# First loads on two queues, a shorter GpSimd chain for the second layer norm, and a new order for all engines

## The chip, the cores and the metric

The kernel runs on one core of a Trainium2 chip. The metric is the device time of one execution in microseconds (us). In the traces and below, PE is the matrix engine (TensorE; its weight loads are shown apart as PEld), DVE is VectorE, ACT is ScalarE, POOL is GpSimd, and SP is the engine that issues most of the transfers. An entry such as "SPq" or "ACTq" is that engine's transfer queue.

## The reference, cut to what matters

One transformer layer over 2048 tokens of width 640, in bfloat16. The first half is linear attention with 32 heads of 20 columns. Its feature map is a softmax of `p` beside a softmax of `-p`, where `p` is q or k times a small weight for each head.

```python
x = A_x
h = x + attention(layernorm(x), wqkv, w_phi, wo)
h2 = h + silu(layernorm(h) @ w1) @ w2          # 640 -> 1728 -> 640

def attention(x, wqkv, w_phi, wo):
    q, k, v = split(x @ wqkv)                  # 32 heads of 20
    phi(y)  = concat(softmax(y @ w_phi), softmax(-(y @ w_phi)))   # 40 features
    kv, z   = phi(k).T @ v, sum(phi(k))        # over all 2048 tokens
    return ((phi(q) @ kv) / (phi(q) @ z + 1e-6)) @ wo
```

The sum `kv` over all tokens cuts the work in two: no query can be finished before the last key is done.

## The kernel before, in words

The 2048 tokens are 16 tiles of 128, numbered t = 0 to 15. Nothing loops: the whole program is one list of words, `ORDER`, and every engine issues its instructions in the order in which the words stand there. A word is an operation and its arguments. `kp.1@2` is the key projection of tile 1 into the PSUM banks from bank 2 on; PSUM has 8 banks, and an operation that takes a bank waits until what lay there has been read out. A letter at the end picks an engine: `a` is ACT and `v` is DVE for a copy or a normalisation; `s` and `a` pick SP's or ACT's queue for a load; for `kn`, `p` gives the whole tile to POOL, `q` three quarters and `b` half, the rest going to DVE.

The start. `lx`, `lk`, `lv`, `lp` load tiles of x, chunks of the key weight, the value weight and the small weight (line 233). `wm` are matmuls on zeros without use for the result (L261). `wt.c` transposes chunk c of the key weight on PE (L312), `wc.c` copies it out (L166 on DVE, L168 on ACT), `fk.c` multiplies it with the small weight (L327), and `fc.c` copies the product to `Wfk`. All five chunks have to be there before a `kp` can end. `lq`, `gk`, `gc` are the same for the query weight, with transposing loads (L248). `st` (L266, L267) and `rs` (L270 to L279) give mean and reciprocal deviation of a tile, `xn` the normalised tile (L287 on DVE, L292 on ACT). It is transposed either by PE (`xt`, L298, copied out by `xc`) or by a transposing transfer on SP (`xd`, L305).

Stage one, tiles in any order: `vp` and `kp` project (L360, ten matmuls each), `vc` copies v out (L168), `ke` takes exp(p) and exp(-p) on ACT (L385), `kr` sums and inverts on DVE (L393, L396), `kn` normalises (L403 on POOL, L407 on DVE), `cc` accumulates kv in bank 7 (L416). `kc`, `km` and `mt` turn kv into a block-diagonal matrix.

Stage two: `qp.g.i` projects queries of four tiles (L447, ten matmuls of 512 columns, five where i is 2), `qe` takes the exponentials (L457). `dp.t` multiplies with kv (L482), always into four banks; `dw.t` reads them out on DVE in four instructions (L495, L496, L498, L501), `dr` inverts (L506), `do` divides, half a tile at a time, on POOL or DVE (L512), `td` transposes (L532), `op` projects (L539), `oa` adds x on DVE with the row sums (L548). The second layer norm is `sq` (squares and their sums on ACT, L556), `sr` (a chain of one-column steps on POOL, L561 to L569), `hn` (L575), and `hd`, the transposing transfer (L595).

Stage three: for groups of 2, 4, 4, 4 and 2 tiles, `up` projects to 1728 columns (L610, L620), `ua` is the silu on ACT (L632), `yp` and `yh` project back (L656, L669), and `yo` adds the residual and stores (L677, L681). The last tile, 13, is stored in two parts, `yz` (L686).

Of the kernel before, what the change touches and what calls it, by code (L numbers as in the profile page):

```python
# [8 lines left out]
AF = mybir.ActivationFunctionType  # L9
ALU = mybir.AluOpType  # L10
# [8 lines left out]
F32 = mybir.dt.float32  # L19
# [3 lines left out]
WHERE = {t: (g, i) for g, ts in enumerate(GROUPS) for i, t in enumerate(ts)}  # L23

ORDER = """
mo lx.0.1.s st.0 lk.2.3.s wm.512@7 wm.512@7 wm.512@7 wm.512@7 wm.512@7 wm.512@7 wt.2@0 lp.a mk ph lk.3.4.s
wm.256@2 wm.256@2 wm.256@2 wt.3@1 ta wc.2.a wc.3.a lx.1.2.s wm.256@4 wm.256@4 wm.256@4 fk.2@2 lk.0.1.s
wt.0@4 fc.2.a fk.3@6 fc.3.a st.1 rs.0.1 xn.0.v lk.1.2.s wt.1@5 xt.0@0 xc.0.a lk.4.5.s wt.4@1 wc.0.v fk.0@2
fc.0.a wc.1.v fk.1@6 wc.4.v fk.4@4 lx.2.4.s rs.1.2 xn.1.v st.2 xt.1@0 lx.12.16.s st.12 fc.1.a lv.0.3.s st.13
fc.4.a wm.256@1 wm.256@1 wm.256@1 wm.256@1 kp.0@2 xc.1.a kp.1@6 lv.3.5.s rs.2.3 xn.2.a xt.2@1 lx.8.12.s  # L30
lx.4.8.s ke.0 lh.s rs.12.14 xn.12.a xd.12 xn.13.a st.14 vp.1@4 vc.1.a ke.1 xc.2.v kp.2@2 vp.2@0 ke.2 vc.2.a
st.15 rs.14.16 st.8 st.9 xn.15.v xd.13 rs.8.10 xn.9.a vp.0@4 kp.12@6 ke.12 kp.13@2 xn.14.v st.5 st.4 rs.4.6
xn.5.a vc.0.a st.11 xd.15 vp.15@0 lq.3.s vc.15.a xd.14 kp.15@6 ke.15 vp.12@4 l1.2.s xn.4.a vc.12.a vp.13@0
vc.13.a vp.14@6 st.10 rs.10.12 st.7 st.6 rs.6.8 ke.13 xn.11.v xd.11 gk.3@4 xn.10.v xd.5 xd.10 vc.14.a
kp.14@0 kr.1 lq.1.s ke.14 mc gc.3.a xn.7.a xn.6.a kr.0 vp.5@2 vc.5.a kn.1.p vp.10@6 st.3 kp.11@0 vp.11@4
xd.9 kp.5@2 xn.8.a vc.11.a rs.3.4 xn.3.a kr.13 kr.14 vc.10.a kr.12 kp.10@4 kn.0.q cc.0 ke.5 kn.13.q cc.13
ke.11 kr.15 cc.1 kn.14.p cc.14 xd.4 kp.4@2 kn.15.p kr.5 kn.5.b xt.3@6 ke.10 xd.8 vp.8@0 kp.8@4 xc.3.a ke.4
vc.8.a lq.2.s kr.11 xd.6 vp.6@2 vc.6.a kr.2 lq.0.s gk.0@0 kr.4 ke.8 cc.5 kn.12.q gc.0.a kr.8 cc.15 kn.11.p
vp.9@2 vc.9.a kn.4.p xd.7 kp.7@4 ke.7 kr.7 gk.1@0 kn.8.q gc.1.a vp.4@2 vc.4.a kn.2.p kp.9@4 ke.9 kr.9 kn.9.b
lq.4.s gk.4@0 gc.4.a kr.10 vp.7@2 vc.7.a cc.4 cc.8 vp.3@4 vc.3.a gk.2@0 gc.2.a kp.3@2 ke.3 kr.3 kp.6@4 ke.6  # L40
lo.s qp.0.2@6 qe.0.2 qp.0.0@0 qe.0.0 qp.0.1@2 qe.0.1 kr.6 cc.9 l2.4.8.s kn.7.p cc.7 kn.10.b cc.10 kn.3.p
cc.3 cc.2 cc.12 cc.11 kn.6.q cc.6 mt close qp.1.0@4 kc l2.0.4.s km.1 km.0 dp.1@0 qp.2.0@6 dw.1 dr.1 do.1.0.p
dp.2@0 qe.1.0 do.1.1.p td.1 dw.2 dr.2 l1.1.s do.2.0.p qp.1.1@4 qe.2.0 qe.1.1 dp.0@0 dw.0 do.2.1.p dr.0
do.0.1.p qp.1.2@6 qe.1.2 op.1@4 td.2 oa.1 sq.1 dp.3@0 dw.3 do.0.0.p sr.1 hn.1.v td.0 dr.3 hd.1 do.3.0.p
do.3.1.p l1.0.s qp.3.1@6 qe.3.1 qp.2.2@4 dp.4@0 qe.2.2 qp.3.2@5 qe.3.2 dw.4 op.0@6 td.3 oa.0 sq.0 sr.0
dp.6@0 dw.6 op.2@4 oa.2 qp.2.1@6 qe.2.1 hn.0.v hd.0 dp.5@0 dw.5 dr.5 do.5.0.p do.5.1.p l2.8.13.s td.5
qp.3.0@4 qe.3.0 dr.6 do.6.1.p op.3@6 oa.3 dr.4 do.4.0.p do.4.1.p td.4 up.0.3@0 sq.3 sr.3 ua.0.3 dp.7@2 dw.7
up.0.2@6 ua.0.2 do.6.0.p dr.7 do.7.0.v dp.9@0 dw.9 op.5@4 oa.5 up.0.0@6 sq.2 sr.2 hn.2.v td.6 dp.8@0 dw.8
dr.8 hd.2 ua.0.0 up.0.1@4 ua.0.1 hn.3.v op.4@6 dr.9 oa.4 do.8.0.p sq.4 do.8.1.p op.6@0 oa.6 do.7.1.p td.7
sq.5 sr.5 dp.10@2 dw.10 dr.10 sr.4 hd.3 yp.0.0@6 td.8 hn.4.v hd.4 yp.1.1@0 do.10.1.p hn.5.v op.7@2 oa.7 sq.7  # L50
yp.1.0 yh.0.0 hd.5 do.9.1.v do.9.0.p yo.1 dp.13@2 yp.0.1 dw.13 dr.13 do.10.0.p sq.6 td.9 sr.6 up.1.5@0 yo.0
ua.1.5 op.8@2 sr.7 hn.7.v hn.6.v oa.8 do.13.1.p do.13.0.v td.13 op.9@4 up.1.0@6 ua.1.0 oa.9 dp.15@0 dw.15
sq.8 sr.8 hn.8.v dr.15 do.15.0.v do.15.1.v hd.6 sq.9 sr.9 hn.9.v hd.9 up.1.3@4 up.1.6@6 ua.1.3 dp.11@0 dw.11
dr.11 do.11.1.p do.11.0.p ua.1.6 up.1.4@4 ua.1.4 op.13@6 oa.13 dp.12@0 hd.8 up.1.2@4 ua.1.2 dw.12 dr.12 hd.7
up.2.6@6 ua.2.6 dp.14@0 td.15 op.15@4 oa.15 dw.14 dr.14 do.14.1.v do.12.1.v do.12.0.v up.2.5@6 ua.2.5
do.14.0.v up.1.1@4 td.10 op.10@6 td.12 ua.1.1 yp.2.1@0 up.2.3@2 td.11 td.14 oa.10 up.2.4@4 ua.2.4 sq.10
op.14@6 sq.13 oa.14 up.2.0@4 sq.14 sr.14 ua.2.3 op.11@6 oa.11 sq.11 sr.11 up.2.1@2 up.2.2@6 ua.2.2 hn.11.v
sr.10 ua.2.0 yp.2.0 op.12@6 yp.4.1@4 sr.13 ua.2.1 sq.15 hn.13.v sr.15 hd.13 hn.10.v yh.1.0 hd.10 oa.12 sq.12
yh.2.0@2,6 yp.6.0 yp.6.1 yo.6 hn.15.v sr.12 hn.12.v yp.4.0 yp.3.0@2 hd.12 yp.8.0 yo.4 yp.8.1 yo.8 yp.3.1
hn.14.v hd.14 hd.15 yp.7.0@4 yp.7.1 yh.2.1@6 yo.2 yh.1.1@0 yo.3 yp.9.1 yo.7 hd.11 yp.5.0 yp.5.1 up.4.1@2  # L60
yp.9.0 yo.9 up.3.4@4 ua.3.4 yo.5 up.3.3@6 up.3.0@0 ua.3.0 up.3.1@4 ua.3.1 ua.3.3 up.3.6@0 ua.3.6 up.4.2@4
up.3.2@6 ua.3.2 up.4.0@0 ua.4.0 up.3.5@6 ua.3.5 yp.10.1@0 ua.4.1 yp.12.1@6 up.4.3@2 ua.4.3 yh.3.0 yp.12.0
yo.12 ua.4.2 yp.14.1@2 yp.15.1@4 yp.10.0 yo.10 yp.15.0 yh.3.1@6,0,1 yh.4.0 yp.14.0 yo.15 yo.14 yp.11.0
yp.11.1 yo.11 yp.13.0 yz.13.0.a yp.13.1 yz.13.1.a
"""

@with_exitstack
def kernel(
# [11 lines left out]
    nc = tc.nc  # L80

    P = nc.NUM_PARTITIONS
    T = 16
    D = 640
# [9 lines left out]
    EPS = 1e-5  # L94
# [28 lines left out]
    X = persist.tile([P, T, D], BF16, name="X")  # L123
# [33 lines left out]
    sm = ctx.enter_context(tc.tile_pool(name="sm", bufs=8))  # L157
# [14 lines left out]
    def wk2():  # L172
        return late["work"]
# [383 lines left out]

    def op_sr(t):
        st = tl["hst", t]
        m = sm.tile([P, 3], F32, name="hm")  # L560
        nc.gpsimd.tensor_scalar(  # L561
            out=m[:, 0:1], in0=st[:, 0:1], scalar1=1.0 / D, scalar2=0.0, op0=ALU.mult, op1=ALU.add,
        )
        nc.gpsimd.tensor_tensor(m[:, 2:3], m[:, 0:1], m[:, 0:1], op=ALU.mult)  # L564
        nc.gpsimd.tensor_scalar(  # L565
            out=m[:, 1:2], in0=st[:, 1:2], scalar1=1.0 / D, scalar2=EPS, op0=ALU.mult, op1=ALU.add,
        )
        nc.gpsimd.tensor_tensor(m[:, 1:2], m[:, 1:2], m[:, 2:3], op=ALU.subtract)  # L568
        nc.gpsimd.tensor_tensor(m[:, 1:2], m[:, 1:2], nhalf[:, 0:1], op=ALU.pow)  # L569
        tl["hm", t] = m  # L570

    def op_hn(t, eng="v"):
        m = tl["hm", t]
        hn = wk2().tile([P, D], BF16, name="hn", bufs=4)
        nc.vector.tensor_scalar(  # L575
            out=hn[:], in0=X[:, t, :], scalar1=m[:, 0:1], scalar2=m[:, 1:2],
            op0=ALU.subtract, op1=ALU.mult,
        )
        tl["hn", t] = hn

    def op_hp(t):
# [141 lines left out]
```

## Time and profile before

| | us |
|---|---|
| three runs | 238.71, 240.01, 241.31 |
| their median | 240.01 |
| the profiled execution | 239.73 |
| its span, first to last instruction | 238.0 |
| what lies around the span | 1.73 |

The profile shows one execution. PE is busy for 230.1 us of the span, DVE for 140.3, ACT for 110.2 and POOL for 91.0. "Idle" of a group of instructions is the time that its engine stood still just before them, and the arrow names what ended that. Matmuls are pipelined: the end of one overlaps the next, so that time between starts says more of PE than busy time does.

### The profile page before, as it was taken

How to read it: one execution, taken by the hardware profiler on the slowest of the kernel's cores; microseconds unless marked ns; L12 is line 12 of the kernel's file. 1: busy time of each engine (PE TensorE's matmuls, PEld its weight loads, DVE VectorE, ACT ScalarE, POOL GpSimd, SP SyncE). 2: the span in 40 equal slices, each digit the busy share in tenths (PEclk: the TensorE clock that was granted, in tenths of full speed). 3: DMA queues.
4: the chain of work that ended last, by engine and by line, in shares of the span. 5: the costliest groups of instructions: out<-in, count | busy, mean ns of one | idle time of the engine just before them, and what ended most of it. 6: DMA issues, size and time to landing. Idle time of an engine off the chain costs nothing. (4 is left out here: it accounts for less than half of the span.)

```text
span 238.0 us, 6265 instructions
## 1 busy us (share of the span) xinstructions
PE 230.1 (97%) x2657; PEld 149.1 (63%) x2676; DVE 140.3 (59%) x258; ACT 110.2 (46%) x167; POOL 91.0 (38%) x184
## 2 busy tenths in 40 slices
PE   6999999999998999999999999999999999999995
PEld 3877767777464465787555455556776754766662
DVE  4799999999978988898857845122323020001132
ACT  3879988787866566732217322437000013452000
POOL 8446895989933542827624200056100000000000
PEclk9999999999999999999999999999999999999999
DMA  6976957580001896724621512102124310000111
GB/s 175 313 274 128 179 115 108 131 291 3 3 6 27 182 169 124 133 38 59 138 58 32 110 31 55 28 3 50 34 58 110 83 58 0 0 3 0 55 58 56
DMA packets 42813, 20.68 MB, mean 87 GB/s; under 512 B 34336, under 2 KB 42272, under 8 KB 42784
## 3 DMA queue, kind: packets, MB, share of 16 engines
q1 hardware_dynamic: 41840, 20.08, 37.2%
q8 instruction: 21, 0.34, 0.6%
q10 hardware_dynamic: 944, 0.19, 0.4%
q14 instruction: 8, 0.07, 0.1%
HBM read 9.61 MB, written 2.62 MB: 51 GB/s over the span
## 5 line engine op out<-in xcount | busy, mean ns | idle before, releaser
L632 ACT ACTIVATE shT<-mm 128x1024 bf16<-128x1024 f32 (+2 forms) x29 | 27.3, 963 | 73.6 <-PE mm L610 69.1
L610 PE MATMUL mm<-HnT,w 128*128 128x512 bf16 (+1 forms) x316 | 58.8, 335 | 0.7 <-DMA HnT<-hn 0.2
L656 PE MATMUL mm<-w,shT 128*128 128x320 bf16 (+2 forms) x415 | 58.5, 299 | 0.1
L656 PEld LDWEIGHTS <-shT 128*128 128x128 bf16 x416 | 39.7, 98 | 17.4 <-issue 1.1
L610 PEld LDWEIGHTS <-w 128*128 128x128 bf16 x325 | 31.3, 98 | 23.6 <-issue 1.1
L677 DVE TENSOR_TENSOR ob<-mm,X 128x640 bf16<-128x640 f32 x15 | 12.1, 819 | 56.5 <-PE mm L656 25.8
L360 PEld LDWEIGHTS <-XnT 128*128 128x128 bf16 x320 | 30.7, 98 | 12.3 <-DMA XnT<-xn 0.7
L403 POOL TENSOR_TENSOR Ek<-Ek,Sk 128x1280 bf16<-128x1280 bf16 (+2 forms) x16 | 33.4, 2110 | 3.7 <-DVE Sk L396 3.6
L512 POOL TENSOR_TENSOR o<-u,rd 128x320 bf16<-128x320 f32 x23 | 16.4, 736 | 21.6 <-DVE rd L506 16.2
L539 PE MATMUL mm<-wo,ot 128*128 128x320 bf16 x160 | 24.1, 299 | 0.1
L360 PE MATMUL mm<-wv,XnT 128*128 128x320 bf16 x160 | 23.7, 299 | 0.4 <-DMA XnT<-xn 0.4
L360 PE MATMUL mm<-Wfk,XnT 128*128 128x320 bf16 x160 | 23.7, 299 | 0.0
L457 ACT ACTIVATE EqT<-mm 128x1024 bf16<-128x1024 f32 (+1 forms) x24 | 19.6, 885 | 8.7 <-PE mm L447 8.7
L393 DVE TENSOR_REDUCE Sk<-Ek 128x64 f32<-128x1280 bf16 x16 | 23.2, 1450 | 0.5 <-ACT Ek L385 0.5
L548 DVE SCALAR_TENSOR_TENSOR X<-mm,X 128x640 bf16<-128x640 f32 x16 | 13.2, 823 | 16.5 <-PE mm L539 16.5
L447 PE MATMUL mm<-XnT,Wfq 128*128 128x512 bf16 x91 | 22.0, 379 | 0.8 <-issue 0.5
L385 ACT ACTIVATE Ek<-mm 128x640 bf16<-128x640 f32 x32 | 20.6, 707 | 2.5 <-PE mm L360 1.5
L539 PEld LDWEIGHTS <-ot 128*128 128x128 bf16 x160 | 15.3, 98 | 7.6 <-PE mm L447 0.5
L556 ACT ACTIVATE sq<-X 128x640 bf16<-128x640 bf16 x16 | 11.8, 736 | 12.1 <-DVE X L548 9.4
L447 PEld LDWEIGHTS <-Wfq 128*128 128x128 bf16 x100 | 9.2, 98 | 10.1
L266 DVE BATCH_NORM_STATS2 stats<-X 128x6 f32<-128x320 bf16 x32 | 13.6, 467 | 3.0 <-DMA X<-in_A_x_dram 3.0
L498 DVE TENSOR_TENSOR u<-mm,w 128x672 f32<-128x672 f32 x16 | 13.7, 857 | 1.1 <-DVE w L496 0.3
(75 smaller groups left out, 208.3 us busy)
## 6 DMA issues: line engine op xcount, KB each, us to landing
out_dram<-ob SPq DMA_DIRECT2D x15, 160.0 KB, 1.8
w<-in_B_w_dram SPq DMA_DIRECT2D x3, 720.0 KB, 5.5
X<-in_A_x_dram SPq DMA_DIRECT2D x3, 640.0 KB, 8.1
w<-in_B_w_dram SPq DMA_DIRECT2D x2, 640.0 KB, 7.8
wk<-in_A_wqkv_dram SPq DMA_DIRECT2D x5, 160.0 KB, 3.6
wo<-in_A_wo_dram SPq DMA_DIRECT2D x1, 800.0 KB, 5.5
w<-in_B_w_dram SPq DMA_DIRECT2D x1, 800.0 KB
wv<-in_A_wqkv_dram SPq DMA_DIRECT2D x1, 480.0 KB, 7.7
```

Of the source, the lines that this page charges most:

```text
L360: nc.tensor.matmul(ps[:, half, 0:320], tok(XnT[t // GT], t)[:, c, :], W[:, c, half * 320 : (half + 1) * 320], start=(c == 0), stop=(c == C ...
L385: nc.scalar.activation(Ek[:, s, :].rearrange("p (a n) -> p a n", a=2), tl["kp", t][:, :, 0:320], AF.Exp, scale=1.0 - 2.0 * s,)
L393: nc.vector.tensor_reduce(Sk[:], tl["ek", t][:].rearrange("p s (h f) -> p (s h) f", f=DH), axis=AX.X, op=ALU.add,)
L403: nc.gpsimd.tensor_tensor(Ek3[:, 0:n], Ek3[:, 0:n], Sk[:, 0:n].unsqueeze(2).to_broadcast([P, n, DH]), op=ALU.mult,)
L447: nc.tensor.matmul(ps[:, k, :], Wfq[:, c, r * P : (r + 1) * P], XnT[g][:, c, :], start=(c == 0), stop=(c == C - 1),)
L457: nc.scalar.activation(E[:, s, rs[0] : rs[-1] + 1, :], tl["qp", g, i][:, 0 : len(rs), :], AF.Exp, scale=1.0 - 2.0 * s,)
L498: nc.vector.tensor_tensor(u[:], A[1][:, :, :, 0:21], w[:].unsqueeze(3).to_broadcast([P, 4, 8, 21]), op=ALU.mult,)
L512: (nc.vector if eng == "v" else nc.gpsimd).tensor_tensor(tl["o", t][:, a * 320 : (a + 1) * 320].rearrange("p (h f) -> p h f", f=DH), tl["u ...
L539: nc.tensor.matmul(ps[:, half, 0:320], tl["ot", t][:, c, :], wo[:, c, half * 320 : (half + 1) * 320], start=(c == 0), stop=(c == C - 1),)
L610: nc.tensor.matmul(ps[:, i * W : (i + 1) * W], w1[:, c, fc * P : (fc + 1) * P], HnT[g][:, c, 0:W], start=(c == 0), stop=(c == C - 1), skip ...
L632: nc.scalar.activation(sh[:, a:b], tl["up", g, k][:, 0 : b - a], AF.Silu)
L656: nc.tensor.matmul(ps, shT[g][:, fc * W + i * P : fc * W + (i + 1) * P], w2[:, fc, a:b], start=first and fc == 0, stop=last and fc == FC - ...
```

## The change

The code of three places changes. `sr` now builds eps minus the squared mean before the squares are there, and takes it in as the added scalar of the step that scales the sum of squares; so there are two steps behind the squares in place of three, and five in all as before. `hn` gets a second form on ACT (scale and bias, with one more POOL step for the bias), which the new order uses for tiles 3, 4, 6, 7, 12 and 15. And the order is new for all engines.

```diff
-        m = sm.tile([P, 3], F32, name="hm")
+        m = sm.tile([P, 4], F32, name="hm")
...
         nc.gpsimd.tensor_tensor(m[:, 2:3], m[:, 0:1], m[:, 0:1], op=ALU.mult)
         nc.gpsimd.tensor_scalar(
-            out=m[:, 1:2], in0=st[:, 1:2], scalar1=1.0 / D, scalar2=EPS, op0=ALU.mult, op1=ALU.add,
-        )
-        nc.gpsimd.tensor_tensor(m[:, 1:2], m[:, 1:2], m[:, 2:3], op=ALU.subtract)
+            out=m[:, 2:3], in0=m[:, 2:3], scalar1=-1.0, scalar2=EPS, op0=ALU.mult, op1=ALU.add,
+        )
+        nc.gpsimd.tensor_scalar(
+            out=m[:, 1:2], in0=st[:, 1:2], scalar1=1.0 / D, scalar2=m[:, 2:3], op0=ALU.mult, op1=ALU.add,
+        )
         nc.gpsimd.tensor_tensor(m[:, 1:2], m[:, 1:2], nhalf[:, 0:1], op=ALU.pow)
...
     def op_hn(t, eng="v"):
...
+        if eng == "v":
+            nc.vector.tensor_scalar(
+                out=hn[:], in0=X[:, t, :], scalar1=m[:, 0:1], scalar2=m[:, 1:2],
+                op0=ALU.subtract, op1=ALU.mult,
+            )
+        else:
+            nc.gpsimd.tensor_scalar(
+                out=m[:, 3:4], in0=m[:, 0:1], scalar1=m[:, 1:2], scalar2=-1.0, op0=ALU.mult, op1=ALU.mult,
+            )
+            nc.scalar.activation(hn[:], X[:, t, :], AF.Identity, bias=m[:, 3:4], scale=m[:, 1:2])
```

The order of the start. Before, SP issued every load but that of the small weight; now x of tile 1, the small weight and key chunk 0 come on ACT's queue, and on SP's queue the second load is a double one, tiles 2 and 3 of x.

```diff
-mo lx.0.1.s st.0 lk.2.3.s wm.512@7 wm.512@7 wm.512@7 wm.512@7 wm.512@7 wm.512@7 wt.2@0 lp.a mk ph lk.3.4.s
-wm.256@2 wm.256@2 wm.256@2 wt.3@1 ta wc.2.a wc.3.a lx.1.2.s wm.256@4 wm.256@4 wm.256@4 fk.2@2 lk.0.1.s
-wt.0@4 fc.2.a fk.3@6 fc.3.a st.1 rs.0.1 xn.0.v lk.1.2.s wt.1@5 xt.0@0 xc.0.a lk.4.5.s wt.4@1 wc.0.v fk.0@2
-fc.0.a wc.1.v fk.1@6 wc.4.v fk.4@4 lx.2.4.s rs.1.2 xn.1.v st.2 xt.1@0 lx.12.16.s st.12 fc.1.a lv.0.3.s st.13
-fc.4.a wm.256@1 wm.256@1 wm.256@1 wm.256@1 kp.0@2 xc.1.a kp.1@6 lv.3.5.s rs.2.3 xn.2.a xt.2@1 lx.8.12.s
...
+lx.1.2.a lk.1.2.s lp.a lx.2.4.s lk.0.1.a lk.2.3.s lk.3.4.s lk.4.5.s st.1 ta wm.512@7 wm.512@7 wm.512@7
+wm.512@7 wm.512@7 wm.512@7 wt.1@0 mk ph wc.1.a wm.256@1 wm.256@1 wm.256@1 wm.256@1 wm.256@1 wm.256@1
+wm.256@1 wm.256@1 fk.1@2 rs.1.2 wt.0@1 st.2 rs.2.3 wm.256@5 wt.2@4 xn.1.a wc.2.a wm.256@6 wt.3@5 xt.1@6
+wt.4@7 fc.1.a lx.8.12.s st.3 rs.3.4 wc.0.v fk.0@0 fc.0.a fk.2@2 fc.2.a wc.3.v wc.4.v mo xc.1.v lx.0.1.s
+lv.0.3.s xn.2.v xn.3.v fk.4@4 fc.4.v fk.3@6 lv.3.5.s st.8 xt.2@0 xt.3@1 fc.3.a xc.2.a lx.12.16.s st.0 rs.0.1
+xc.3.a kp.1@2 st.9 st.10 ke.1 lq.2.s xn.0.v kp.2@6 ke.2 rs.8.10 kp.3@4 vp.2@0 vc.2.a xt.0@2 xc.0.a ke.3
+st.11 rs.10.12 lx.4.8.s xn.10.a xn.8.v xd.8 kr.1 kn.1.p vp.3@6 vp.0@0 vc.3.a xn.11.a gk.2@2 vc.0.a vp.1@4
+lq.1.s st.13 gc.2.a vp.8@6 st.12 rs.12.14 vc.8.a mc st.15 xn.9.a st.6 kp.0@0 ke.0 kp.8@2 ke.8 st.5 st.14
+xn.12.a vc.1.a xn.13.v xd.10 kp.10@6 ke.10 xd.11 kp.11@0 ke.11 rs.14.16 st.4 rs.4.6 st.7 xn.15.v rs.6.8 kr.8
+kn.8.p xn.14.v vp.11@2 kr.3 kn.3.p kr.2 lq.4.s gk.4@4 gc.4.a xd.9 kn.2.p xd.13 xn.5.a vp.13@6 lq.3.s kp.13@0
...
```

The first `dp` of stage two, and the end:

```diff
-cc.3 cc.2 cc.12 cc.11 kn.6.q cc.6 mt close qp.1.0@4 kc l2.0.4.s km.1 km.0 dp.1@0 qp.2.0@6 dw.1 dr.1 do.1.0.p
-dp.2@0 qe.1.0 do.1.1.p td.1 dw.2 dr.2 l1.1.s do.2.0.p qp.1.1@4 qe.2.0 qe.1.1 dp.0@0 dw.0 do.2.1.p dr.0
-do.0.1.p qp.1.2@6 qe.1.2 op.1@4 td.2 oa.1 sq.1 dp.3@0 dw.3 do.0.0.p sr.1 hn.1.v td.0 dr.3 hd.1 do.3.0.p
...
-yp.11.1 yo.11 yp.13.0 yz.13.0.a yp.13.1 yz.13.1.a
...
+qe.0.0 cc.14 cc.9 cc.12 cc.4 cc.6 cc.5 cc.15 kc km.0 close km.1 l1.2.s qp.0.2@6 qe.0.2 l2.0.4.s qp.1.2@2
+qe.1.2 dp.0@4 dw.0 dr.0 do.0.0.p qp.1.1@0 qe.1.1 lo.s do.0.1.p td.0 dp.1@2 dw.1 qp.1.0@6 dr.1 do.1.0.p
+dp.2@0 dw.2 dr.2 qe.1.0 qp.3.0@4 qe.3.0 dp.5@0 dw.5 do.1.1.p dr.5 do.5.0.p op.0@6 l2.4.8.s oa.0 qp.2.0@4
+qe.2.0 dp.6@0 do.2.1.v dw.6 td.1 do.2.0.p do.5.1.p td.5 op.1@6 oa.1 sq.0 qp.3.2@4 qe.3.2 sr.0 hn.0.v hd.0
...
+yh.3.0 yo.12 yh.3.1@6,7 yo.11 yp.10.0 yo.10 yp.13.0 yz.13.0.s yp.13.1 yz.13.1.a
```

Counted over both lists, PE's words are the same: the same projections, four `xt`, and `wm` with six times 512 and ten times 256 columns. Between the engines these move: `kn` whole on POOL for 11 tiles (8 before), three quarters for 2 (5 before), half for 3 as before; `xn` on ACT for 9 tiles (10 before); `fc.4` and `vc.14` from ACT to DVE; `do` halves on DVE 12 (9 before); six `hn` from DVE to ACT.

## The prediction

> **What bounds the kernel now.** I read the page's busy shares first, then the table of windows, then PE's timeline in the two places where the windows show slack, and the waits last.
>
> ```profile
> PE 230.1 (97%) x2657; PEld 149.1 (63%) x2676; DVE 140.3 (59%) x258; ACT 110.2 (46%) x167; POOL 91.0 (38%) x184
> ```
>
> PE is busy for 97% of the span, the next engine for 59%. Nothing that leaves PE's work as it is can win much; the question is only how long PE stands still or works on nothing useful.
>
> ```profile
> 0.00:6.00 6.00, 4.18 (x19) 2.25 (x20) 2.52 (x6) 2.18 (x3) 5.00 (x24) 1.00 0.67 176
> 6.00:12.00 6.00, 5.97 (x75) 5.11 (x74) 4.57 (x13) 4.96 (x8) 2.35 (x8) 1.00 0.92 313
> 18.00:24.00 6.00, 6.00 (x46) 4.33 (x45) 5.83 (x19) 6.00 (x11) 3.90 (x11) 1.00 0.61 122
> 24.00:30.00 6.00, 6.00 (x50) 4.40 (x49) 5.81 (x10) 5.71 (x9) 5.04 (x11) 1.00 1.14 177
> 70.00:80.00 10.00, 8.87 (x194) 4.91 (x197) 8.15 (x16) 6.84 (x8) 3.08 (x5) 1.00 0.31 72
> 140.00:180.00 40.00, 39.84 (x255) 24.50 (x256) 13.91 (x29) 11.57 (x19) 7.97 (x30) 1.00 0.18 39
> ```
>
> The columns are the window, its length, the busy time of PE, PEld, DVE, ACT and POOL, the granted clock, the transfer share and GB/s. Slack of PE lies in the first 6 us and at 70 to 80; from 140 to 180 there is none. From 18 to 30 DVE and ACT are as full as PE: there three engines bound the kernel at once.
>
> ```profile
> 6.70 0.81 PE L327 MATMUL mm<-phb,wTk 128*128 128x140 bf16 x6
> 8.78 1.31 PE L327 MATMUL mm<-phb,wTk 128*128 128x140 bf16 x18
> 10.24 0.60 PE L261 MATMUL mm<-warm,ident 128*128 128x256 bf16 x4
> 10.68 0.57 PE L360 MATMUL mm<-Wfk,XnT 128*128 128x320 bf16 x3
> ...
> 73.29 0.46 PE L482 MATMUL mm<-KVBD,EqT 32*128 32x44 bf16 x40 [0.48 <-DVE u L501]
> 73.69 2.33 PE L447 MATMUL mm<-XnT,Wfq 128*128 128x512 bf16 x9
> 76.25 0.46 PE L482 MATMUL mm<-KVBD,EqT 32*128 32x44 bf16 x40 [0.23 <-DVE u L501]
> ```
>
> PE's timeline: busy at the start is not useful. The first `kp` starts at 10.68, and before it PE had only the transposes and small products of five chunks, two tiles of `xt` and matmuls on zeros. Later two `dp` wait until DVE has read the previous one out.
>
> ```profile
> 30.87 2.89 PE L360 MATMUL mm<-wv,XnT 128*128 128x320 bf16 x20 [0.37 <-DMA XnT<-xn]
> 136.25 1.24 PE L610 MATMUL mm<-HnT,w 128*128 128x512 bf16 x5 [0.20 <-DMA HnT<-hn]
> ```
>
> These are the only other two waits of PE over 0.2 us that are marked after the start.
>
> **The change, part by part.** PE's work is equal word for word, so I add up only what PE waits. Sums are made against the profiled execution, 239.73 us, of which 238.0 is the span; it lies 0.28 under the median of 240.01, and inside the three runs.
>
> *The start.* Issuing one load takes SP 0.42 us, the next follows 0.47 later. Before, x of tile 0 lands at 3.3 (DVE's statistics begin at 3.33), the second load at 4.02, x of tile 1 at 5.76 (statistics at 5.78). In the new order x of tile 1 is first on ACT's queue beside a key chunk, first on SP's. Its landing s lies between 3.3, a first load with only the small weight beside it, and 4.0, when two such loads had landed: I take 3.5, nearer to the first, as both begin at once. DVE then sets the pace. From s on: statistics 1.10, `phb` 1.00 (L195), two more statistics 2.10 (for the double tile, wanted at 5.6: before, the third load on SP's queue had landed at 5.35 with 480 KB, what SP's queue moves here up to it, and the fifth at 6.13 with 800 KB, what both queues move; I take the first, since the double tile is issued at 1.25, that load at 1.71), three `wc` of 0.49, one `xc` of 0.44, two `xn` of 0.42, together s + 6.95 = 10.45 us. With 0.45 for `xt` of tile 3, `kp.1` starts at 10.9. PE has then one `xt` more behind it than before at 10.68 (0.32). So 10.9 against 11.0: -0.1, and -0.3 to +0.4 for the two ends of s; the late end of the double tile gives +0.4 as well, not once more, since DVE wants it 2.1 after s. ACT's `fc.3` ends at 10.75 and DVE's `fc.4` at 11.3, for a place in `kp.1` that PE reaches at 11.45. If that cover of 0.15 is gone, PE waits as long as it is late. `fc.4` and `vc.14` on DVE have no row; copying out 640 columns took DVE 0.49 (L166) in two-byte elements and 0.82 (L677) with an addition from four-byte ones; I take 0.75, nearer the latter, as the source is of four bytes too. The three issues on ACT's queue (0.46 each, row of the small weight) push its table load of 1.28 from 1.28 to about 2.2, done at 3.5, and the first `wc` on ACT comes near 5.0: nothing. Ten memsets (`mo`) leave POOL's start; the selection that makes the identity may run 0.2 earlier and PE's first useless matmuls with it, which DVE's pace hides.
>
> The Trainium skill, page "DMA: Bandwidth & Descriptors", section "Issuing engines are not separate DMA queues", speaks against a gain here: transfers from all queues run on the same 16 DMA engines, so a second queue saves only the time of issuing. By that page s would be nearer to 4.0 and the start +0.4 instead of -0.1. The trace of before has only 25 KB on the second queue, so it cannot decide.
>
> *Stage one, 11 to 68 us.* Marked waits are 0.37 at 30.87, which between starts is 0.53, and 0.15 of the `cc` at 67.5 for the last `kn`. The transposed tile waited for comes earlier in the new order, so -0.53; new waits are bounded by 0 and by what ACT could cost (the rival below), and I put 0.3. Loads of ACT: `xn` -0.94, `fc` -0.64, `vc` -0.71, so -2.3 in all. DVE: three `kn` parts less at 1.20 (-3.6), plus 0.75, 0.82 and 0.42, so -1.6. POOL: 3 x (2.39 - 1.93) = +1.4; running sums of the mean rows in the new order put its last `kn` at 65.4, and PE asks for it at 66.9. That cover of 1.5 pays for the added 1.4.
>
> One row to weigh: DVE's part of a `kn` took 0.43 us at 49.88, while POOL had nothing to do, and 1.46 on average for the pair at 36.11, while POOL normalised another tile. The Trainium skill, "SBUF — State Buffer", section "Who interferes with whom", has a DVE instruction with two inputs in SBUF blocked by a GpSimd one that reads SBUF. The trace agrees. At 0.43 apiece DVE would save 1.3 in place of 3.6 and end the stage with +0.7 in place of -1.6; it is not PE's wait in either case.
>
> *The first `dp`.* Before, `dp` starts at 70.08, 73.29 and 76.25. Without a wait it would be 0.40 for a `dp`, 2.13 for ten `qp` matmuls (0.213 each) and 0.10 for switching, 2.63; so the two waits cost 0.58 and 0.33. DVE needs 2.60 and 2.36 from first reading to last (70.63 to 73.23, 73.84 to 76.20). In the new order three pairs have one such `qp` between them and share banks: 0 and 1, 1 and 2, 2 and 5. That is 0.58 + 0.33 + 0.33, hence +0.33. `qe.0.2` now comes after `kc` on ACT, ready about when `dp.0` asks; 0 to 0.4, I take 0. The added wait holds up `qp.1.1`, `qp.1.0` and `qp.3.0`, whose exponentials ACT waits for; ACT idles 0.7 to 1.8 in this place already.
>
> *Second layer norm.* One step less behind the squares is 0.21 (L568) and some 0.07 to the next, 0.28 for each tile; the moved step runs while ACT makes squares. It counts only where PE waits for `HnT`: 0.20 once. With hn of six tiles on ACT (0.94, the row of `xn` there, against 0.49 on DVE, and 0.19 on POOL before it) the chain of these tiles is 0.36 longer in the balance, and SP's transposes (1.2 to 1.3 each) follow later. I counted PE's work between an `op` and the `up` that needs its tile: for tile 4 it is 10.6 us, against oa 0.9, squares 0.95, steps 1.2, hn 0.94, issue and landing 2.65. Even with 1.3 for each of two transposes ahead it fits. Whether ACT has to load a table between silu and this form of hn no row shows; squares and silu alternate before with one load of 1.28 in all, and the form runs beside exp without one. I take none; with a load ahead of it, 1.28, tile 4 would stand at 10.5 of 10.6, and ACT has the room (busy 5.36 of 20 us from 100 to 120). The Trainium skill, "ScalarE: Activation LUTs", section "Table sets: the hidden batching unit", has identity in every table set; no run here shows it. For tile 10 the transposing transfer stands behind the store of tile 7 on SP: 5.2 us of PE against 4.3. That cover of 0.9 is the thinnest here. -0.20, and +0.1 for thin spots around 90 to 130 us, where `op.8` asks for banks about 0.1 after DVE frees them.
>
> *The end.* ACT's queue issues both last stores in 0.84, so the second starts at 235.51 though its data are there at 235.38. The first one moves to SP: -0.13.
>
> The sum: -0.1 - 0.53 + 0.3 + 0.33 - 0.20 + 0.1 - 0.13 = -0.23, and 239.73 - 0.23 = 239.5 us.
>
> **The rivals.** *ACT falls behind in stage one (slower).* Between `vc.2` and `ke.10` of the new order ACT has five `vc`, one `xc`, four `ke`, four `xn` and one `gc`. Packed, as the timeline has them (`ke` 1.24, `xn` 0.87, `vc` 0.60, `gc` 0.70), that is 12.8, from 16.5 to 29.3. PE needs the bank at 29.65: 13 projections of 1.36 and 1.0 of small ones after 10.95. At the mean rows (1.41, 0.94, 0.71, 0.89) it is 14.6, ending at 31.1, so PE waits 1.45. The same race comes again at `kp.14` behind `vc.10`; twice makes 2.9, less the 0.3 already in the sum: 242.1. It decides once ACT is over 0.35 late. For it: ACT was busy 6.00 of 6.00 from 18 to 24. Against: its work falls by 2.3.
>
> *The second queue brings nothing.* s at 4.0, the start +0.4: 240.0.
>
> *All waits go and none comes.* The start -0.3, `dp` -0.91, stage one -0.68, `HnT` -0.20, the end -0.13, so -2.2: 237.5. For it: PE has slack nowhere else. Against: the three pairs of `dp`.
>
> **How the numbers follow.** The forecast has 0.47, ACT's rival 0.29, the second queue's 0.16, the waits gone 0.08. The likeliest gives 239.5, its own range is 238.5 to 240.8. To leave out no more than 2 in 10, the range goes down to 237.9, near the last rival, and up to 242.6, past ACT's 242.1. One per cent, about what a measurement of this kernel can tell from no change, is 2.4 us on 240.01, so 237.6 and 242.4. Faster by more needs nearly every wait gone: 0.06. Slower by more is a little over half of ACT's rival: 0.17. Within it 0.77.
>
> **What would show it.** Start: `kp.1` near 10.9, and DVE without idle time from 5.6 to 10.4. Stage one: no wait over 0.3 of PE's L360 on ACT. `dp`: three waits marked by u L501. `HnT`: none. The end: one store on each queue. The forecast is wrong if PE's L360 waits for `ke` or `vc`, if x of tile 1 lands past 4.0, or if an `up` waits for a transposing transfer over 0.5.

## The result, and the profile after

| | before | after |
|---|---|---|
| median, us | 240.07 (six runs, 238.71 to 241.5) | 246.36 (six runs, 245.93 to 247.86) |
| the profiled execution | 239.73 | 246.2 |
| its span | 238.0 | 244.5 |

The ratio is 1.027, with a 95% interval of 1.0218 to 1.0323. The forecast was 239.5, within 237.9 to 242.6: the kernel is slower by 6.3, and none of the cases in the prediction reaches that far. In three of the experiments below one execution was far off (301.34, 829.65 and 269.09 us: one accumulation apart, the short chain, two accumulations forward); it raises the medians given there by 0.08 to 0.23 us and is left out of the ratios.

The page's busy shares, and the windows in the form shown of the kernel before:

```profile
PE 232.5 (95%) x2676; PEld 149.2 (61%) x2676; DVE 139.1 (57%) x255; ACT 114.0 (47%) x170; POOL 93.3 (38%) x187
```

```profile
0.00:6.00 6.00, 4.42 (x19) 2.31 (x20) 2.15 (x5) 2.18 (x3) 3.06 (x14) 1.00 0.72 215
6.00:12.00 6.00, 4.18 (x63) 3.54 (x63) 5.93 (x14) 3.97 (x6) 4.48 (x18) 1.00 1.05 389
50.00:60.00 10.00, 6.33 (x44) 3.99 (x45) 4.76 (x6) 2.57 (x5) 4.96 (x3) 0.83 0.82 297
70.00:80.00 10.00, 9.20 (x362) 5.25 (x360) 6.91 (x11) 5.95 (x9) 2.31 (x4) 1.00 0.01 3
140.00:180.00 40.00, 40.00 (x293) 23.70 (x292) 11.48 (x22) 15.90 (x25) 10.64 (x34) 1.00 0.23 45
```

Two rows are new: from 6 to 12 PE works 4.18 rather than 5.97, and from 50 to 60, where the prediction expected nothing, 6.33 of 10, at a granted clock of 0.83. At 140 to 180 all is full, as forecast. The kernel before had from 50 to 60:

```profile
50.00:60.00 10.00, 10.00 (x144) 7.38 (x143) 9.39 (x11) 7.68 (x15) 9.80 (x5) 1.00 0.24 86
```

The first place, all engines on the timeline (start, length, engine, instructions, idle time before them):

```profile
9.72 2.18 DVE L287 TENSOR_SCALAR xn<-X,MV,RS 128x640 bf16<-128x640 bf16 x2
...
9.85 1.52 POOL L204 MEMSET Vp<- 128x32 bf16 x10
...
11.61 0.80 PE L298 MATMUL mm<-ident,xn 128*128 128x128 bf16 x10 [1.28 <-DVE xn L287]
...
12.24 4.24 PE L360 MATMUL mm<-Wfk,XnT 128*128 128x320 bf16 x30
```

Two `xn` take DVE 2.18 in place of the 0.84 that the prediction counted, the first of them alone 1.83, and the ten memsets of `mo`, which the new order puts here, run on POOL at the same time. `kp.1` starts at 12.24 and not at 10.9: +1.34.

The second place, PE's timeline:

```profile
48.23 1.46 PE L416 MATMUL mm<-Ek,Vp 128*21 128x40 bf16 x150
53.67 0.28 PE L416 MATMUL mm<-Ek,Vp 128*21 128x40 bf16 x10 [3.98 <-issue]
53.88 5.48 PE L360 MATMUL mm<-Wfk,XnT 128*128 128x320 bf16 x30
```

The five accumulations `cc.11`, `cc.10`, `cc.13`, `cc.0` and `cc.2` stand together, 160 small matmuls. After 150 of them, in the middle of `cc.2`, PE does nothing for 4.17 (from the start of one matmul to that of the next), and the releaser is "issue": the profile shows no data and no bank that is waited for. Then thirty matmuls of 320 columns take 5.48, which took 4.24 above: the granted clock stands at 0.5 from 53.0 to 56.4, and that is +1.24. So 239.5 + 1.34 + 4.17 + 1.24 = 246.25, and the execution took 246.2. All else comes out near the forecast in sum, but not term by term: a further gap of 0.53 of the same kind, at 71.56 in the run of eight `cc`, is in it, so that the match to 0.05 is luck.

What PE may wait for in such a gap shows in the table of queues:

```profile
q8 instruction: 21, 0.34, 0.6%
```

The 21 packets have 16,384 bytes each, and PE has 5,368 records, so there is one for about 256 of its instructions. Late in this trace, from 143.95 on, six packets start 123 to 131 matmuls apart, each matmul with its weight load, which is the same count. One of the 21 is on its way from 51.17 to 52.28; PE goes on 1.39 after its end.

### The profile page after: what moved, and what is told of

The parts are those of the page before. It is cut to its first block, busy times and chain, and to the rows that moved or that the text cites. A ratio compares the mean times of both kernels' runs of the same rounds, so it can differ in the third digit from the quotient of the medians.

```text
span 244.5 us, 6321 instructions
## 1 busy us (share of the span) xinstructions
PE 232.5 (95%) x2676; PEld 149.2 (61%) x2676; DVE 139.1 (57%) x255; ACT 114.0 (47%) x170; POOL 93.3 (38%) x187
## 4 chain that ended last, share of the span: by engine, by line
PE 80%; DVE 11%; DMA 3%; issue 3%; ACT 0%; ACTq 0%; DVEq 0%
PE mm L618 23%; PE mm L664 23%; PE mm L360 11%; PE mm L539 8%; PE mm L447 6%; DVE stats L266 4%; PE mm L482 3%; PE mm L416 2%; DMA XnT<-xn 2%; DMA phr<-in_A_w_phi_dram 2%; PE mm L628 1%; PE mm L677 1%; DVE u L498 1%; DVE u L501 1%; DVE MV L267 1%
## 5 line engine op out<-in xcount | busy, mean ns | idle before, releaser
L360 PEld LDWEIGHTS <-XnT 128*128 128x128 bf16 x320 | 31.4, 99 | 12.9 <-DMA XnT<-xn 0.3
L403 POOL TENSOR_TENSOR Ek<-Ek,Sk 128x1280 bf16<-128x1280 bf16 (+2 forms) x16 | 34.7, 2193 | 8.1 <-DVE Sk L396 6.8
L512 POOL TENSOR_TENSOR o<-u,rd 128x320 bf16<-128x320 f32 x20 | 15.0, 771 | 27.8 <-DVE rd L506 21.4
L360 PE MATMUL mm<-Wfk,XnT 128*128 128x320 bf16 x160 | 24.1, 309 | 0.0
L360 PE MATMUL mm<-wv,XnT 128*128 128x320 bf16 x160 | 23.4, 299 | 0.1
L447 PE MATMUL mm<-XnT,Wfq 128*128 128x512 bf16 x100 | 23.3, 380 | 0.2 <-ACT EqT L457 0.2
```

The lines of the kernel that those rows point to most:

```text
L360: nc.tensor.matmul(ps[:, half, 0:320], tok(XnT[t // GT], t)[:, c, :], W[:, c, half * 320 : (half + 1) * 320], start=(c == 0), stop=(c == C ...
L403: nc.gpsimd.tensor_tensor(Ek3[:, 0:n], Ek3[:, 0:n], Sk[:, 0:n].unsqueeze(2).to_broadcast([P, n, DH]), op=ALU.mult,)
L447: nc.tensor.matmul(ps[:, k, :], Wfq[:, c, r * P : (r + 1) * P], XnT[g][:, c, :], start=(c == 0), stop=(c == C - 1),)
```

## The experiments

The theory: (a) the memsets hold up DVE's `xn`; (b) small matmuls use up PE's instructions faster than they are brought, so that many in a row run PE dry; (c) the halved clock follows from standing still. Rivals for (b): the big loads of SP's queue, which the new order bunches there (three parts of `w` and `wo` issued from 47.8 to 50.5), hold the instructions up whatever stands there; or `cc.2` waits for its data. All runs are compared with the kernel before on the same chip. Line numbers are one less where the order takes one line less.

**The memsets early.** One word of the changed kernel moves:

```diff
-fc.2.a wc.3.v wc.4.v mo xc.1.v lx.0.1.s
+fc.2.a wc.3.v wc.4.v xc.1.v lx.0.1.s
...
-wt.1@0 mk ph
+wt.1@0 mo mk ph
```

> Of the changed kernel, only the ten memsets on POOL move: they stand before the mask at the start, as they did in the kernel before, and no longer behind the row statistics of tile 3. Theory 1 (the memsets hold up DVE): in the changed kernel the normalisation of tile 2 on DVE took 1.83 us while POOL wrote the ten memsets, and that of tile 3 only 0.43 behind them; without them both take about 0.42, the first key projection starts near 10.9 instead of 12.24, and the kernel takes 1.3 us less than the changed one, about 245. Rival 2 (DVE was late for another reason, such as the statistics it waits for): the first takes as long as before and the first key projection stays near 12.2, no gain.

Measured: 245.84, ratio 1.024 [1.0187, 1.0292]. The timeline:

```profile
9.90 0.79 DVE L286 TENSOR_SCALAR xn<-X,MV,RS 128x640 bf16<-128x640 bf16 x2
...
11.04 3.15 PE L359 MATMUL mm<-Wfk,XnT 128*128 128x320 bf16 x22
```

The two `xn` take 0.79 and `kp.1` starts 1.20 earlier. In the profiled execution, 246.08, it is lost again in the second place: the window from 50 to 60 has

```profile
50.00:60.00 10.00, 7.78 (x45) 4.61 (x46) 3.75 (x4) 2.01 (x4) 4.74 (x3) 0.66 0.70 255
```

a clock of 0.66, which is 6.8 at one half in place of 3.4. The gap before it is 3.83, at the same matmul. The other three executions, 245.0 to 245.86, have a mean clock of 0.993, as with one halved stretch of 3.4, and their median, 245.82, is 0.3 below that of the changed kernel's four with such a clock; where the rest of the 1.20 went in them no trace shows.

**The big loads later.** In the changed kernel `lo` goes behind `td.0`, and three parts of `w` behind `td.5` and `hd.1`:

```diff
-kp.6@2 l2.8.13.s ke.9
+kp.6@2 ke.9
...
-km.1 l1.2.s qp.0.2@6 qe.0.2 l2.0.4.s qp.1.2@2
+km.1 qp.0.2@6 qe.0.2 qp.1.2@2
...
-qe.1.1 lo.s do.0.1.p td.0
+qe.1.1 do.0.1.p td.0 lo.s
```

> Of the changed kernel, the four big weight loads that SP issues at 47.8 to 50.5 us (two parts of w2, one of w1, and wo, 2.96 MB) move behind transposing transfers of stage two, so that none is in flight at 47 to 57 us. In the changed kernel PE stands still for 4.0 us in the middle of one accumulation of kv, at its 22nd matmul of 32, where no data can be missing; a 16 KB instruction transfer starts at 51.17, ends at 52.28, and PE goes on at 53.67. Theory A (the instruction transfer stands behind the big loads): the gap shrinks to under 1 us, the clock stays at 1.0, the kernel takes 4 to 5 us less, 241 to 242. Theory B (five accumulations in a row use up 320 instructions in 1.3 us, faster than any transfer of instructions brings the next ones, whatever else moves): the gap stays over 3 us and the time near 246.

Measured: 248.63, ratio 1.038 [1.0311, 1.0448]. The window, and PE's timeline:

```profile
50.00:60.00 10.00, 7.63 (x59) 4.94 (x60) 6.87 (x8) 5.28 (x9) 7.39 (x4) 1.00 0.01 2
...
52.37 0.24 PE L415 MATMUL mm<-Ek,Vp 128*21 128x40 bf16 x10 [2.53 <-issue]
52.55 4.25 PE L359 MATMUL mm<-Wfk,XnT 128*128 128x320 bf16 x30
...
85.56 2.82 PE L538 MATMUL mm<-wo,ot 128*128 128x320 bf16 x10 [2.70 <-DMA wo<-in_A_wo_dram]
```

With transfers at a share of 0.01 from 50 to 60 the gap is still 2.72 between starts. So the loads make about 1.4 of its 4.17, and the run of small matmuls the rest. This shorter gap halves no clock: 4.25 for thirty. The new loss is `wo`, which comes 2.70 late to `op.0`, with the clock halved behind it (0.91 on average from 80 to 100).

**The accumulations apart.** Three of the five go between the projections that follow; the loads stay:

```diff
-kr.5 cc.13 cc.0 vc.15.a cc.2 kp.9@0 lh.s xd.6 kp.6@2 l2.8.13.s ke.9 kr.9 kp.4@4 ke.4
+kr.5 vc.15.a kp.9@0 lh.s xd.6 kp.6@2 cc.13 l2.8.13.s ke.9 kr.9 kp.4@4 cc.0 ke.4
...
-qp.0.1@0 qe.0.1
+qp.0.1@0 cc.2 qe.0.1
```

> Of the changed kernel, three of the five accumulations of kv that stand together before the projection of tile 9 move one by one behind the next projections (behind kp.6, kp.4 and qp.0.1); the big loads stay. Theories A and B both have the gap go, if PE has not used up its instructions before about 53.7: 320 dense instructions are spread over 5 us. The gap at 49.5 is under 0.5, the clock stays at 1.0 and the time falls by 5.3 (4.0 of gap and some 1.3 of halved clock behind it) to about 241. Rival C (PE waits for something that the trace does not name, belonging to the projection of tile 9): the gap stays, now ahead of that projection.

Measured: 241.35, ratio 1.0052 [1.0019, 1.0086], 5.0 less than the changed kernel.

```profile
50.00:60.00 10.00, 10.00 (x157) 6.27 (x156) 9.55 (x11) 7.71 (x12) 9.90 (x6) 1.00 0.83 300
```

PE works 10.00 of 10 at full clock while the transfers run at a share of 0.83, the changed kernel's 0.82. This falls on the side of (b): loads alone stop nothing.

**One accumulation apart.** Only `cc.2`, the last of the five, goes behind `qp.0.1`:

```diff
-kr.5 cc.13 cc.0 vc.15.a cc.2 kp.9@0
+kr.5 cc.13 cc.0 vc.15.a kp.9@0
...
-qp.0.1@0 qe.0.1
+qp.0.1@0 cc.2 qe.0.1
```

> The changed kernel with one word moved: cc.2, last of the five accumulations in a row, goes behind qp.0.1, two projections and a half later. Theory (dense small matmuls run PE dry; big loads on the queues only make the bringing later): the same matmul in PE's count, 22 matmuls past the fourth accumulation, is then reached after some 2.2 more projections of 1.36, 3.0 later, so the gap falls from 4.1 to about 1.1, the clock isn't halved, and the kernel takes about 246.2 - 3.0 - 1.26 = 241.9, with 241.4 to 243.5 as bounds. Rival (the big loads hold up PE's instructions whatever stands there): the gap stays at 3 to 4 and the kernel at 245 to 246. Rival (cc.2 itself waits for its data): the gap goes with cc.2 to its new place.

Measured: 242.09, ratio 1.0077 [1.0039, 1.0115]. PE's timeline:

```profile
50.02 3.16 PE L359 MATMUL mm<-Wfk,XnT 128*128 128x320 bf16 x22
53.92 1.26 PE L359 MATMUL mm<-Wfk,XnT 128*128 128x320 bf16 x8 [0.74 <-issue]
```

The gap now lies in the middle of a projection of keys that waits for nothing of `cc`, and it is the same matmul in PE's count: 22 past `cc.0`. Between starts it is 1.04; 1.1 was expected. Neither `cc.2`'s data nor its kind sets the place, only the count. The packet ends at 52.53, again 1.39 before PE goes on.

**Memsets early and the three apart.**

```diff
-wt.1@0 mk ph
+wt.1@0 mo mk ph
...
-kr.5 cc.13 cc.0 vc.15.a cc.2 kp.9@0 lh.s xd.6 kp.6@2 l2.8.13.s
+kr.5 vc.15.a kp.9@0 lh.s xd.6 kp.6@2 cc.13 l2.8.13.s
...
```

`cc.0` and `cc.2` go behind `kp.4` and `qp.0.1`, as above.

> Both edits: memsets first, and the three accumulations apart. If the two causes are all that made the changed kernel slow, the gains add: 1.3 + 5.3 = 6.6 less than the changed kernel, 239.6, within 0.5 of the kernel before. If they share one cause, or another wait takes their place, it is less than the sum: over 241.

Measured: 240.34, ratio 1.0014 [0.9984, 1.0045]. These two edits, four words moved, give back 6.0 of the 6.3; all the rest of the change together is worth nothing that can be told from zero. `kp.1` starts at 11.21. A smaller gap of the same kind is left in the run of eight `cc` ahead of the first `dp`:

```profile
66.27 1.04 PE L415 MATMUL mm<-Ek,Vp 128*21 128x40 bf16 x110 [0.54 <-issue]
```

**One queue for the first loads**, on top of the last kernel:

```diff
-lx.1.2.a lk.1.2.s lp.a lx.2.4.s lk.0.1.a
+lx.1.2.s lk.1.2.s lp.a lx.2.4.s lk.0.1.s
```

> Of the kernel with the memsets early and three accumulations moved, x of tile 1 and key chunk 0 go from ACT's queue back to SP's; only the small weight stays on ACT's. The prediction's own step: x of tile 1 lands where nothing is beside it, s = 3.3 in place of the 3.94 that two queues gave, the key chunks and the double tile follow 0.47 apart and later than now. If the start hangs on x of tile 1, kp.1 comes at 10.6 in place of 11.21 and the kernel takes 239.7. Rival: the double tile and the key chunks are late instead (two more issues of 0.47 ahead of the last chunk), kp.1 comes at 11.2 to 12.1 and the kernel takes 240.3 to 241.2. If all queues only share one bandwidth and the issue time is what a second queue saves, it is the rival that holds.

Measured: 240.48, ratio 1.0005 [0.9973, 1.0037]: no difference. DVE's and PE's timelines:

```profile
3.39 0.89 DVE L265 BATCH_NORM_STATS2 stats<-X 128x6 f32<-128x320 bf16 x2 [2.20 <-DMA X<-in_A_x_dram]
...
6.22 0.89 DVE L265 BATCH_NORM_STATS2 stats<-X 128x6 f32<-128x320 bf16 x2 [0.83 <-DMA X<-in_A_x_dram]
...
10.97 2.20 PE L359 MATMUL mm<-Wfk,XnT 128*128 128x320 bf16 x15
```

x of tile 1 is there at 3.39, 0.6 earlier than on two queues, and DVE then stands still for 0.83 until the double tile comes at 6.22. `kp.1` comes at 10.97, in kernels with memsets early and the first loads on two queues at 10.96 to 11.21. The start does not hang on x of tile 1 but on what comes last, and the number of queues hardly moves that.

**The short chain and the end by themselves**, in the kernel before (`sr` as in the change, and `yz.13.0.a` to `yz.13.0.s`):

> The kernel before, with nothing changed but the shorter chain behind the squares (two steps in place of three) and the first of the two last stores on SP's queue. Prediction: the wait of 0.20 for HnT at 136.25 goes, and 0.13 at the end, 239.73 - 0.33 = 239.4 profiled, 239.7 in the median, a ratio of 0.9985 that this measurement can hardly tell from 1. Rival: the transposing transfer sets that wait and the end is set by the landing of the last store alone, so both stay and the ratio is 1.000. Either way it says how much of the prediction's small terms is real, by the two places in the trace.

Measured: 240.64, ratio 1.001 [0.997, 1.0051]. In the trace the wait for `HnT` is gone, and the last store is issued 0.03 after its data rather than 0.13. But this execution has a wait of 1.58 of `op.1` at 79.00, a place that the edit does not touch, so such small terms are there in the trace and lost in the spread. The releaser named is ACT's `qe`, but the trace's semaphore records show another: `op.1` needs 16 completions of the transposing transfer of `ot`, of which 15 come at 77.25 to 77.39 and the last at 78.92, while in the kernel before all 16 come at 77.73 to 77.88. An instruction packet was on its way from 76.82 to 77.84; whether it held up the sixteenth part is not shown.

**Two accumulations forward**, on top of memsets early and three apart:

```diff
-kp.15@2 ke.15 kr.15 vp.12@0 vc.12.a
+kp.15@2 cc.7 ke.15 kr.15 vp.12@0 cc.9 vc.12.a
...
-mt cc.7 qe.0.0 cc.14 cc.9 cc.12
+mt qe.0.0 cc.14 cc.12
```

> Of the kernel with the memsets early and three accumulations moved, two accumulations of the run of eight ahead of the first dp go forward, cc.7 behind kp.15 and cc.9 behind vp.12, so that six stand in a row in place of eight. Theory (small matmuls in a row use up PE's instructions faster than they are brought): PE comes to the place where it ran dry for 0.54 to 0.73 at 66.27 later in work, the gap goes, nothing else changes: 239.7 against 240.34. Rival: the gap is the wait for the last kn or for a bank and not for instructions; it stays with the same length at the same accumulation, 240.3, or the moved accumulations wait for their kn and add up to 1.

Measured: 239.86, ratio 0.9968 [0.9938, 0.9998]. The six `cc` run through without a gap. The test is weaker than it looks: with one queue the run of eight had only 0.15 of idle time at that matmul, since its packet had ended 0.33 earlier (64.52 against 64.85). The same kernel again:

> The kernel with memsets early, three accumulations apart and two forward once more, for a second interval, since its first one, 0.9938 to 0.9998 against the kernel before, ends close to 1. If it is faster than the kernel before: a ratio of 0.996 to 0.998, 239.2 to 239.9. If the first interval was chance: a ratio of 1.000.

Measured: 239.84, ratio 0.9978 [0.9946, 1.0011]. It is the best version found, at most a little better than the kernel before: one interval ends below 1, the other just above. With one queue for the first loads:

> Of the kernel with memsets early, three accumulations apart and two forward, x of tile 1 and key chunk 0 go back to SP's queue, as was tried before without the two forward. If the earlier landing of x of tile 1 counts to the end, kp.1 starts at 10.97 in place of 11.2 and the kernel takes 239.86 - 0.24 = 239.6. Rival: what is won at the start is lost again at the wait near 29.5, where PE waits for transposed tiles that SP issues behind more loads; then it is 239.9.

Measured: 240.22, ratio 1.0004 [0.9979, 1.0029]; no gain, as the rival said, but not for its reason: `kp.1` came only at 11.27, so nothing was won at the start that could be lost later.

**The six `hn` on DVE**, in the best version:

```diff
-sr.3 hn.3.a sq.8 hd.5
+sr.3 hn.3.v sq.8 hd.5
...
-hn.4.a hd.4 yh.0.0 do.15.0.p dw.9 dr.9
+hn.4.v hd.4 yh.0.0 do.15.0.p dw.9 dr.9
```

and the same for tiles 6, 7, 12 and 15.

> Of the kernel with memsets early, three accumulations apart and two forward, all six hn that the change moved to ACT go back to DVE. The prediction took the move for nothing: no PE wait and no table load. Then it makes no difference here either, 239.9 within 0.4. Rival 1: on ACT they lengthen the chain of HnT by 0.94 + 0.27 - 0.49 each and hold up a projection somewhere; then DVE is faster by 0.2 to 0.7, 239.2 to 239.7. Rival 2: DVE then has 6 x 0.49 = 2.9 us more in a stretch where PE waits for the banks that DVE reads out, and the kernel is slower by 0.5 to 1.5, 240.4 to 241.4.

Measured: 244.22, ratio 1.0153 [1.0107, 1.0198], more than any theory had. DVE's timeline, PE's, and a window:

```profile
110.58 0.80 DVE L577 TENSOR_SCALAR hn<-X,hm 128x640 bf16<-128x640 bf16 x2 [1.20 <-POOL hm L570]
112.47 0.84 DVE L577 TENSOR_SCALAR hn<-X,hm 128x640 bf16<-128x640 bf16 x1 [1.08 <-POOL hm L570]
```

```profile
115.63 0.46 PE L481 MATMUL mm<-KVBD,EqT 32*128 32x44 bf16 x40 [2.70 <-DVE u L500]
```

```profile
116.00:118.00 2.00, 2.00 (x21) 1.18 (x9) 1.83 (x5) 0.00 (x0) 0.00 (x0) 0.53 0.48 91
118.00:120.00 2.00, 2.00 (x11) 1.21 (x9) 1.54 (x3) 0.00 (x0) 0.70 (x2) 0.61 0.00 0
```

DVE's own work is not too much. The `hn` wait for POOL's steps, and `dw.9` stands behind them in DVE's order, so PE gets its banks 2.70 late, and then runs at half clock for 1.88 + 1.56 = 3.4, which costs half of that: 2.70 + 1.7 = 4.4, the loss. Two of the six executions, 242.49 and 242.54, have a mean clock of 0.998 and 0.999 and lose some 2.7, the wait alone. Put to the test with only the two in front of `dw.9`, those of tiles 3 and 4, back on ACT:

> Of the kernel with memsets early, three accumulations apart and two forward, four hn (tiles 6, 7, 12, 15) on DVE, those of tiles 3 and 4 on ACT as in the change; with all six on DVE it took 244.2, with none 239.9. Theory: not DVE's load but its order is what cost 4.3 there: the hn of tiles 3 and 4 stand ahead of dw.9 and wait 1.20 and 1.08 for POOL's chain, dw.9 waits behind them, and PE 2.70 for its bank, after which the clock is halved. With these two on ACT that place is as it was, so 239.9, at most 240.5. Rival: DVE has too much to do from 100 to 180 us; with four of six moved back, 4/6 of 4.3 = 2.9 comes back and the kernel takes 242.8.

Measured: 239.96, ratio 0.9975 [0.9946, 1.0003]. The place decides, not the load.

## Why the prediction was wrong, step by step

*"PE's work is equal word for word, so I add up only what PE waits."* This is the step that failed. It took PE's instructions to be there whenever data and banks are. In the new order the same 512 `cc` matmuls stand closer, five in a row at 48.2, and the instructions for the place where PE then stands still come 4.17 late. The move of `cc` and that of the big loads on SP's queue were not priced at all; they cost 5.0, shown by setting three words apart. In the kernel before at most four `cc` stand together in that part, and its one longer run came late enough after its packet, 63.68 to 64.64:

```profile
65.34 2.01 PE L416 MATMUL mm<-Ek,Vp 128*21 128x40 bf16 x226
```

None of the three signs that the prediction gave for being wrong came: no L360 waited for `ke` or `vc`, x of tile 1 landed before 4.0, and no `up` waited. They watched only the waits that it had priced.

*The ten memsets, "which DVE's pace hides".* Only the place that they left was looked at, not the one where they went: on DVE's path to `kp.1`. That is 1.34, and 1.20 of it went when they moved. The prediction had the rule at hand, and used it for `kn` alone. The Trainium skill, page "SBUF — State Buffer", section "Who interferes with whom", lists `tensor_scalar` among the forms of DVE that can, in a two-port mode, lock out GpSimd or be locked out for a whole instruction. The trace agrees in kind: 1.83 for an `xn` beside memsets, 0.42 without. In size it is more than one instruction: the 1.41 are nearly all ten memsets, 1.52.

*The halved clock* had no term. The Trainium skill, "TensorE: Matmul & The Clock Gate", section "HAM oscillation — how this bites in real kernels", warns of idle gaps over about 3.4 us. Here 4.17 halved it for 3.4 and 3.83 for 6.8; a wait of 2.70 halved it too (the `hn` on DVE, and `wo` late), but a gap of 2.72 between starts did not. The measurements decide: the limit is no sharp one at 3.4. The traces show what does decide. From the first clock record on, every complete stretch at one clock lasts a whole multiple of 3.413: 14, 1 and 55 times in the changed kernel, 13, 2 and 55 with memsets early, 23, 1 and 46 with the loads later, 32, 1 and 36 with the `hn` on DVE. So the clock was set anew every 3.413. In the 3.413 ahead of these four halved stretches PE stood still for 3.33, 2.19, 2.82 and 2.70; the most idle time in such a period at full clock that no halved one followed is 1.67, in the wait of `op.1` above. The gap of 2.72 fell on both sides of such a border, 1.41 and 1.12. The gap of 3.83 did too, but with 2.19 and 1.45, and there the clock, halved by the first part, stayed so for another 3.413. The mean clocks differ from execution to execution: of the six of the changed kernel the two longest, 247.72 and 247.86, have a mean clock of 0.986, as for two halved stretches, and the others 0.992 or 0.993, as for one.

*The start.* s was taken at 3.5 and measured at 3.94, near the late end, as by the page "DMA: Bandwidth & Descriptors" of the Trainium skill, which the prediction weighed against it. But the +0.4 that hung on s did not follow: with s = 3.39 on one queue the start is the same within 0.3. Where the memsets are out of the way `kp.1` comes at 10.96 to 11.27, against 10.9 forecast. The late end of the double tile, 6.2, is real on one queue, where it takes the place of s; on two it had landed at 4.94. What the sum did not have is a wait of `phb` for the small weight, second on ACT's queue: 0.27 with memsets early and the three apart.

*Stage one.* The rival that ACT falls behind did not come: no projection of this stage waits for ACT. The wait of 0.53 goes, and one of about 0.29 stands ahead of the `vp` at 31.10, against the 0.3 put in for new ones: as forecast.

*The first `dp`.* Three waits marked by DVE's last reading were forecast, and three came, in PE's timeline of the changed kernel:

```profile
79.09 0.45 PE L482 MATMUL mm<-KVBD,EqT 32*128 32x44 bf16 x38 [0.43 <-DVE u L501]
...
82.11 0.45 PE L482 MATMUL mm<-KVBD,EqT 32*128 32x44 bf16 x38 [0.17 <-DVE u L501]
...
85.13 0.47 PE L482 MATMUL mm<-KVBD,EqT 32*128 32x44 bf16 x40 [0.30 <-DVE u L501]
```

Marked they are 0.90 together, where the kernel before has 0.48 + 0.23 = 0.71. Between starts, which is how the prediction counted, they cost more: the `qp` in front start at 76.21, 79.48 and 82.50 and the `op` behind the last `dp` at 85.52, so with 2.63 for each pair without a wait it is 0.64 + 0.39 + 0.39 = 1.42 against 0.91: +0.51, not +0.33.

*Second layer norm and the end.* No wait for `HnT`, as forecast. `hn` on ACT needs no table load: there is one load for silu in the whole trace. But the move was not worth nothing. It was taken as a chain 0.36 longer; what it does is take two waits of 1.20 and 1.08 out of DVE's order, without which this order would lose 4.4 (2.7 where the clock is not halved). At the end the last store is issued 0.03 after its data, in the changed kernel too, where it was 0.13: a gain of 0.10 for the 0.13 forecast.

So the small terms came out close: 239.5 forecast, and 240.34 with the two causes removed, of which 0.54 is a further gap of the first kind. The error is two terms that were not in the sum, and what the clock made of one of them.

## What to carry to other kernels

Look at how the instructions stand on an engine, not only at their sum: on PE, many short matmuls in a row (here it stopped after 150 in 1.46 us) are a risk even when all data are there, and putting longer ones between them cost nothing here. A step that is moved must be priced where it goes, against every engine beside it, and an instruction that waits, against what stands behind it on its engine. A wait of PE that leaves it idle for 2.2 us or more of one 3.4 us period can cost half of 3.4 us on top; between 2.2 and, by estimate, 4.4 us (twice 2.2, split evenly) it is luck whether it does, so price it as a chance and look at more than one execution.

## What the runs showed of the hardware that was not expected

PE's instructions come in packets of 16 KB, one for some 256 instructions. In the cases where PE ran dry it went on 1.24 to 1.51 after the end of a packet: 1.39 in the changed kernel, 1.39 with one accumulation apart, 1.51 with the loads later, 1.24 to 1.43 in the run of eight. The place in the run of eight lies 256 matmuls behind the first, 512 instructions with the weight loads, or two packets. That the packets are what PE waited for is inferred from these times and counts; that the place goes by PE's count is shown by one accumulation set apart. What sets the time at which a packet is asked for was not settled: it started at 49.48 with the loads out of the way and at 51.17 with them, for the same matmul. Ten memsets of 0.15 each on POOL held one DVE instruction for nearly the time of all ten. The granted clock was set anew every 3.413, halved after 2.19 or more of idle time in one such period and not after 1.67 or less.
